# A gated-attention and MLP kernel on one core: a whole-sequence decay pass with a scheduled pipeline, rewritten as six hand-ordered rounds of four units with paired heads

## The chip, the core and the metric

The kernel runs on one core of a Trainium2 chip. The engines named in the profile are PE (matrix multiply; PEld is its weight load), DVE (vector), ACT (activation functions), POOL and SP; SP and POOL also issue the DMAs here. The metric is the device time in microseconds (us). The timed runs of the kernel before gave 297.84, 298.85 and 299.3 us, a median of 298.85 us.

## The reference

```python
batch, n_heads, seq, head_dim = (4, 8, 768, 48)
...
for t in range(S):
    state = alpha[:, :, t, :, None] * state + np.einsum('bhd,bhe->bhde', k[:, :, t], v[:, :, t])
    y[:, :, t] = np.einsum('bhd,bhde->bhe', q[:, :, t], state)
...
x = np.ascontiguousarray(attn_out.transpose(0, 2, 1, 3)).reshape(B * S, H * D)
h = x @ w_in                       # [3072, 384] @ [384, 2048]
g = 0.5 * h * (1.0 + np.tanh(c * (h + 0.044715 * h * h * h)))
return (g @ w_out).astype(np.float32)
```

All inputs and the output are float32. A gated recurrence per batch entry and head is followed by a two-layer MLP with a tanh-GELU on 3072 tokens.

## The kernel before

A unit is 128 time steps of one batch entry, all eight heads: 6 chunks x 4 batch entries = 24 units. Four units with the same chunk form a group, which is 512 tokens for the MLP. Within a unit the recurrence is turned into matmuls. The running sum of log alpha (cum) is a matmul with a triangle of ones; q is scaled by exp(cum), k by exp(-cum); at = k' q' is masked by the triangle (atm); y is atm times v plus q' times the state; and the state moves on as (state + k' v) times the decay of the whole chunk (bend).

**First pass.** For all 24 units, in pairs, POOL issues the alpha loads (L105, rows of 192 bytes in DRAM), ACT takes Ln (L108), PE makes cumla and the chunk's decay (L114, and eight one-column matmuls at L118), DVE stores cum_all (L120) and ACT takes Exp for bend_all (L121). The MLP weights are loaded as float32 by SP and cast by DVE (L127, L159).

**Second pass.** Stage a issues q, k and v on POOL (L190). Stage b takes two Exp on ACT (L200, L202), scales q and k on DVE (L205, L206), casts v on ACT (L208), transposes each head of q and k on PE (L213, L214) and copies both out (L215 ACT, L216 DVE). Stage c does at (L234), the mask (L237, DVE), y (L241, L243), k'v (L245), the state update (L249, L250, DVE), the copy of y to bfloat16 (L255, ACT), its transposes (L259) and their copy (L260, DVE). The MLP of a group is cut into sixteen layer-1 pieces (three matmuls at L275 and a Gelu at L279) and four layer-2 pieces (sixteen matmuls at L286, a copy at L291, a store by SP at L293); up to seven pieces are handed out after each unit.

The program's recording layer sets the order on each engine from this code: it may move an instruction ahead of others by their readiness, and it places the activation-table loads (ACT_TABLE_LOAD) where the function changes between Ln, Exp and Gelu. Each engine then runs its own list strictly in order. A tile pool hands out buffers in turn, and a tile waits until the last reader of its buffer is done.

## Time and profile before

| | |
|---|---|
| median of three timed runs | 298.85 us |
| profiled execution, first to last instruction (the span) | 295.8 us |
| the profiled execution's own time beyond that span | not listed; 298.85 - 295.8 = 3.05 us is the median's distance |
| busy: PE, ACT, DVE, POOL | 224.5, 200.8, 141.3, 87.4 us |
| DMA: read and written | 25.17 and 4.72 MB |
| TensorE clock granted, mean | 0.998 |

A row of instruction groups has the line, engine, operation, tiles (out<-in), sizes and count, then the busy time, the mean of one in ns, the idle time just before them, and what ended most of it. A row of the timeline has start and length in us, engine, line, tiles and count; matmuls are pipelined, so eight in a row take far less than eight times the mean of one. A row of waits has the waiting instruction, what it waited for, the total in us, the number and the longest. A row of a DMA queue has packets, MB, and the time of its packets as a share of sixteen DMA engines in the stretch shown.

### The profile page before, as it was taken

The numbers are of one execution on the slowest core, as the hardware profiler recorded it, in microseconds if no ns is written. First come the engines' busy times: TensorE is split into PE (matmuls) and PEld (weight loads), VectorE is DVE, ScalarE is ACT, GpSimd is POOL, SyncE is SP. The second block draws the span as 40 slices with busy tenths as digits, with TensorE's granted clock in tenths as the row PEclk, the third lists the DMA queues.
The fourth block names the chain that finished last, engine by engine and source line by source line (L and its number), as shares of the span: only waits on it lengthen the run. The fifth ranks groups of instructions, "written<-read, shape, count | busy, mean of one in ns | idle before, by whom it ended". The sixth has DMA issues, their size and how long they took to land.

```text
span 295.8 us, 5241 instructions
## 1 busy us (share of the span) xinstructions
PE 224.5 (76%) x2112; PEld 132.8 (45%) x2112; DVE 141.3 (48%) x274; ACT 200.8 (68%) x301; POOL 87.4 (30%) x114
## 2 busy tenths in 40 slices
PE   0043333332778989899998999999999999999983
PEld 0022212221656535556556555565456644554441
DVE  7183433222599855567548144656243633540011
ACT  0257787978677999996999999945761276304800
POOL 9643321005988758153333213220000000000000
PEclk9999999999999999999999999999999999999999
DMA  7999951002999979373232512241001100011011
GB/s 278 283 187 274 291 126 53 0 1 67 193 187 187 189 144 198 89 181 99 80 82 59 182 53 55 53 109 53 2 1 55 53 2 0 3 53 55 0 53 54
DMA packets 12168, 30.22 MB, mean 102 GB/s; under 512 B 2032, under 2 KB 7152, under 8 KB 11760
## 3 DMA queue, kind: packets, MB, share of 16 engines
q0 software_dynamic: 6144, 18.88, 30.4%
q1 hardware_dynamic: 6000, 11.01, 11.0%
q8 instruction: 16, 0.26, 0.4%
q14 instruction: 8, 0.07, 0.1%
HBM read 25.17 MB, written 4.72 MB: 101 GB/s over the span
## 4 chain that ended last, share of the span: by engine, by line
PE 47%; ACT 34%; DMA 7%; DVE 6%; issue 3%; POOL 1%; SPq 0%; DVEq 0%; POOLq 0%; ACTq 0%
PE acc L286 16%; PE hT L275 15%; ACT gT L279 6%; ACT L279 5%; ACT L108 4%; DMA w_in_f<-in_moe_w_in_dram 4%; ACT qT_ring L215 3%; PE kT_ps L214 3%; PE qT_ps L213 3%; ACT la L108 3%; PE at_ps L234 2%; ACT L200 2%; ACT L202 2%; ACT L121 2%; DVE w_in_sb L127 2%
## 5 line engine op out<-in xcount | busy, mean ns | idle before, releaser
L275 PE MATMUL hT<-xT_all,w_in_sb 128*128 128x512 bf16 x288 | 74.5, 379 | 4.0 <-ACT gT L279 3.8
L286 PE MATMUL acc<-w_out_sb,gT 128*128 128x384 bf16 x384 | 70.8, 326 | 3.0 <-DVE ot L291 2.8
L279 ACT ACTIVATE gT<-hT 128x512 bf16<-128x512 f32 x96 | 55.5, 598 | 16.3 <-PE hT L275 14.2
L286 PEld LDWEIGHTS <-gT 128*128 128x128 bf16 x384 | 36.4, 97 | 28.0 <-issue 4.0
L114 PE MATMUL cumla<-la,ut 128*128 128x384 bf16 x24 | 11.6, 485 | 48.3 <-ACT la L108 39.1
L291 DVE COPY ot<-acc 128x384 f32<-128x384 f32 x24 | 13.3, 555 | 53.6 <-PE acc L286 53.6
L237 DVE TENSOR_TENSOR atm<-at_ps,ut 128x512 bf16<-128x512 f32 x48 | 31.1, 683 | 15.9 <-PE at_ps L234 15.7
L275 PEld LDWEIGHTS <-w_in_sb 128*128 128x128 bf16 x288 | 24.8, 97 | 26.3 <-issue 5.5
L118 PEld LDWEIGHTS <-la 128*48 128x48 bf16 x192 | 9.5, 129 | 55.5 <-issue 55.5
L190 POOL DMA_DIRECT2D q<-in_q_dram x24 | 21.2, 884 | 44.1 <-PE cumla L118 24.1
L120 DVE CAST cum_all<-cumla 128x384 f16<-128x384 f32 x24 | 13.3, 556 | 32.5 <-PE cumla L118 32.5
L190 POOL DMA_DIRECT2D v<-in_v_dram x24 | 21.2, 885 | 25.3 <-ACT v8b L208 21.8
L105 POOL DMA_DIRECT2D a<-in_alpha_dram x24 | 21.5, 900 | 21.3 <-ACT la L108 18.9
L215 ACT COPY qT_ring<-qT_ps 64x1024 bf16<-64x1024 bf16 x24 | 24.1, 1005 | 4.9 <-PE qT_ps L213 4.6
L190 POOL DMA_DIRECT2D k<-in_k_dram x24 | 21.2, 885 | 18.3 <-DVE kp_ring L206 17.4
L208 ACT CAST v8b<-v 128x384 bf16<-128x384 f32 x24 | 12.3, 512 | 18.7 <-PE yps L243 17.9
L216 DVE COPY kT_ring<-kT_ps 64x1024 bf16<-64x1024 bf16 x24 | 16.3, 680 | 17.5 <-PE kT_ps L214 17.1
L108 ACT ACT_TABLE_LOAD x11 | 14.1, 1283 | 13.4 <-DMA a<-in_alpha_dram 13.2
L213 PE MATMUL qT_ps<-ident,qp_ring 128*64 128x128 bf16 x192 | 18.3, 230 | 5.9 <-DVE qp_ring L205 5.3
L205 DVE TENSOR_TENSOR qp_ring<-q,b 128x384 bf16<-128x384 f32 x24 | 13.2, 551 | 14.6 <-PE at_ps L234 5.7
L213 PEld LDWEIGHTS <-qp_ring 128*64 128x64 bf16 x192 | 12.7, 114 | 16.5 <-issue 14.9
L255 ACT CAST x_sb<-yps 128x384 bf16<-128x384 f32 x24 | 11.4, 476 | 12.7 <-PE yps L243 10.6
(49 smaller groups left out, 319.2 us busy)
## 6 DMA issues: line engine op xcount, KB each, us to landing
a<-in_alpha_dram POOLq DMA_DIRECT2D x24, 192.0 KB, 7.2
q<-in_q_dram POOLq DMA_DIRECT2D x24, 192.0 KB, 5.3
k<-in_k_dram POOLq DMA_DIRECT2D x24, 192.0 KB, 5.7
v<-in_v_dram POOLq DMA_DIRECT2D x24, 192.0 KB, 5.2
out_dram<-ot SPq DMA_DIRECT2D x24, 192.0 KB, 1.9
w_in_f<-in_moe_w_in_dram SPq DMA_DIRECT2D x3, 1024.0 KB, 7.4
w_out_f<-in_moe_w_out_dram SPq DMA_DIRECT2D x4, 768.0 KB, 12.4
```

The source lines that it names most:

```text
L105: nc.gpsimd.dma_start(a8[:, i], alpha[b].rearrange("h s d -> s h d")[tsl])
L108: nc.scalar.activation(la8, a8, AF.Ln, scale=float(math.exp(-MU)))
L120: nc.vector.tensor_copy(cum_all[:, tt, :], cumla)
L190: nc.gpsimd.dma_start(t_sb, t_dram[b].rearrange("h s d -> s h d")[tsl])
L213: nc.tensor.transpose(qT_ps[:, h, :], qp[:, h, :], ident)
L215: nc.scalar.copy(qT[0:64], qT_ps)
L216: nc.vector.tensor_copy(kT[0:64], kT_ps)
L237: nc.vector.tensor_tensor(atm, at_ps, ut[:, None, :].to_broadcast([C, 4, C]), op=ALU.mult)
L275: nc.tensor.matmul(hT, w_in_sb[:, j, nt * C:(nt + 1) * C], xsl, start=(j == 0), stop=(j == NKT - 1),)
L279: nc.scalar.activation(gT[:, nt, :], hT, AF.Gelu_apprx_tanh)
L286: nc.tensor.matmul(acc, gT[:, nt, mt * C:(mt + 1) * C], w_out_sb[:, nt, :], start=(nt == 0), stop=(nt == NFT - 1),)
L291: nc.vector.tensor_copy(ot, acc)
```

## The change

The two passes become one. Six groups run in turn through two phases each. In phase A of group g, the layer-2 pieces of group g-1 (sixteen quarter pieces of four matmuls) are interleaved with the attention output of group g (yk) and with the decays of group g+1 (Ln, cum, Exp, scaling). In phase B, the sixteen layer-1 pieces of group g are interleaved with the transposes and the at matrices of group g+1. A helper, _merge, spreads the side work over the main pieces, and the recording layer is told to keep the written order (manual_schedule).

Heads go in pairs: two heads, padded from 48 to 64 columns, fill 128 partitions. A transpose handles two heads (eight per unit in place of sixteen); the two at matmuls of a pair use rows 0-63 and 64-127 of the array; the state of a pair is block diagonal, so q'-state and k'v are four matmuls of 96 columns per unit. Ln and Exp are taken for two units at once and share one table, loaded once per group. v and both weight matrices are cast to bfloat16 by the DMA (on POOL), so the casts on ACT and DVE go away. The first two groups' alpha, q and k are loaded by SP; later groups' by POOL, all in one place, at the start of phase A two groups ahead. PSUM: one two-bank buffer ("ca") for cum and at, two banks ("yk") for transposes, k'v and y, four ("ff") for the MLP.

```diff
-            for pi in range(0, len(units), 2):
...
-    for step in range(NU + 2):
...
+    with ExitStack() as ctx, tc.manual_schedule():
+        _Kernel(ctx, tc, q, k, v, alpha, moe_w_in, moe_w_out, out).run()
...
+def _merge(main, side, first=0.0, last=1.0):
+    lo, hi = first * n, last * n
+    at = [lo + (hi - lo) * (i + 0.5) / m for i in range(m)] if m else []
+    j = 0
+    for i in range(n):
+        while j < m and at[j] <= i:
+            side[j]()
+            j += 1
...
+        self.state = [[const.tile([C, H // 2, 2 * D], BF16, name=f"st{b}_{i}") for i in range(2)]
+                      for b in range(B)]
+        self.NR = 4
+        self.la_ring = [const.tile([C, 2, H, 64], F16, name=f"la{i}") for i in range(self.NR)]
...
+            nc.gpsimd.memset(t[:, :, :, D:64], 0.0)
...
+    def load(self, names, pair, eng):
+        for n in names:
+            dt = F32 if n != "v" else BF16
+            t = self.ld.tile([self.C, 2, self.H, self.D], dt, tag=n + "8", bufs=6 if n == "v" else 4, name=n + "8")
+            for i, (c, b) in enumerate(pair):
+                sl = slice(c * self.C, (c + 1) * self.C)
+                e = eng if n != "v" else self.nc.gpsimd
+                e.dma_start(t[:, i], self.src[n][b].rearrange("h s d -> s h d")[sl])
+                self.u.setdefault((c, b), {})[n] = t[:, i]
+            self.u[pair[0]][n + "pair"] = t
...
+        self.nc.gpsimd.dma_start(
+            self.w_in[:, :, sl], self.w_in_dram.rearrange("(j c) n -> c j n", c=self.C)[:, :, sl])
...
+        self.nc.scalar.activation(self.la_ring[r][:, :, :, 0:self.D], u0["apair"], AF.Ln)
...
+        cum = u0["cum"] = self.ps.tile([self.C, 2, 512], F32, tag="ca", name="cum")
+        for i in range(2):
+            nc.tensor.matmul(cum[:, i, 0:H * D], self.ut_h, la[:, i, :, 0:D], start=True, stop=True)
+            for p in range(H // 2):
+                nc.tensor.matmul(cum[:, i, H * D + p:H * D + p + 1],
+                                 la[:, i, 2 * p:2 * p + 2, :].rearrange("t h d -> t (h d)"),
+                                 self.ones, start=True, stop=True, skip_group_check=True)
...
+        b8 = self.wk.tile([self.C, 2, H * D], BF16, tag="b8", name="b8")
+        binv8 = self.wk.tile([self.C, 2, H * D], BF16, tag="binv8", name="binv8")
+        bend = self.grp.tile([self.C, 2, H // 2], F32, tag="bend", bufs=6, name="bend")
+        nc.scalar.activation(b8, cum[:, :, 0:H * D], AF.Exp)
+        nc.scalar.activation(binv8, cum[:, :, 0:H * D], AF.Exp, scale=-1.0)
+        nc.scalar.activation(bend, cum[:, :, H * D:H * D + H // 2], AF.Exp)
+        qp, kp = self.qp_ring[r], self.kp_ring[r]
+        nc.vector.tensor_tensor(qp[:, :, :, 0:D], u0["qpair"],
+                                b8.rearrange("t i (h d) -> t i h d", h=H), op=ALU.mult)
+        nc.vector.tensor_tensor(kp[:, :, :, 0:D], u0["kpair"],
...
+            ps = self.ps.tile([C, 2, H // 2, C], BF16, tag="yk", bufs=2, name="qkT_ps")
+            for j, s in enumerate((u["qp"], u["kp"])):
+                for p in range(H // 2):
+                    nc.tensor.transpose(
+                        ps[:, j, p, :], s[:, 2 * p:2 * p + 2, :].rearrange("t h d -> t (h d)"), self.ident)
+            nc.vector.tensor_copy(t, ps)
...
+        at = self.ps.tile([C, 2, H // 2, C], F32, tag="ca", name="at")
+        for p in range(H // 2):
+            for o in range(2):
+                sl = slice(64 * o, 64 * o + 64)
+                nc.tensor.matmul(at[:, o, p, :], kT[sl, p, :], qT[sl, p, :], start=True, stop=True)
+        atm = u["atm"] = self.grp.tile([C, 2, H // 2, C], BF16, tag="atm", bufs=6, name="atm")
+        for o in range(2):
+            nc.vector.tensor_tensor(atm[:, o], at[:, o],
+                                    self.ut[:, None, :].to_broadcast([C, H // 2, C]), op=ALU.mult)
...
+        kv = self.ps.tile([C, H // 2, 2 * D], F32, tag="yk", bufs=2, name="kv")
+        for p in range(H // 2):
+            nc.tensor.matmul(kv[:, p, :], u["kp"][:, 2 * p:2 * p + 2, :].rearrange("t h d -> t (h d)"),
+                             u["v"][:, 2 * p:2 * p + 2, :].rearrange("t h d -> t (h d)"),
+                             start=True, stop=True)
+        for o in range(2):
+            ps, fs = slice(64 * o, 64 * o + 64), slice(D * o, D * o + D)
+            acc = kv[ps, :, fs]
+            if c > 0:
+                s = self.wk.tile([C, H // 2, D], F32, tag=f"stmp{o}", name="stmp")
+                nc.vector.tensor_tensor(s[ps], acc, old[ps, :, fs], op=ALU.add)
+                acc = s[ps]
+            nc.vector.tensor_tensor(new[ps, :, fs], acc,
+                                    u["bend"][ps, :, None].to_broadcast([64, H // 2, D]), op=ALU.mult)
...
+        yps = self.ps.tile([C, H, D], F32, tag="yk", bufs=2, name="yps")
+        if c > 0:
+            st = self.state[b][c % 2]
+            for p in range(H // 2):
+                nc.tensor.matmul(yps[:, 2 * p:2 * p + 2, :], u["qT"][:, p, :], st[:, p, :],
+                                 start=p == 0, stop=False, skip_group_check=True)
+        for h in range(H):
+            nc.tensor.matmul(yps[:, h, :], u["atm"][:, h % 2, h // 2, :], u["v"][:, h, :],
+                             start=c == 0, stop=True, skip_group_check=True)
+        x = self.wk.tile([C, H * D], BF16, tag="x", name="x")
+        nc.scalar.copy(x, yps.rearrange("t h d -> t (h d)"))
...
+            ps = self.ps.tile([C, self.NKT, C], BF16, tag="yk", bufs=2, name="xT_ps")
+            for j in range(self.NKT):
+                nc.tensor.transpose(ps[:, j, :], x[:, j * C:(j + 1) * C], self.ident)
+            nc.vector.tensor_copy(xT[:, :, i, :], ps)
...
+            h = self.ps.tile([C, N * C], F32, tag="ff", bufs=4, name="hT")
+            for j in range(self.NKT):
+                nc.tensor.matmul(h, self.w_in[:, j, nt * C:(nt + 1) * C],
+                                 xT[:, j].rearrange("p g t -> p (g t)"),
+                                 start=j == 0, stop=j == self.NKT - 1)
+            nc.scalar.activation(gT[:, nt, :], h, AF.Gelu_apprx_tanh)
...
+                acc[mt] = self.ps.tile([C, self.d_model], F32, tag="ff", bufs=4, name="acc")
+            for nt in range(part * 4, part * 4 + 4):
+                nc.tensor.matmul(acc[mt], gT[:, nt, mt * C:(mt + 1) * C], self.w_out[:, nt, :],
+                                 start=nt == 0, stop=nt == self.NFT - 1)
+            if part == self.NFT // 4 - 1:
+                ot = self.wk.tile([C, self.d_model], F32, tag="ot", name="ot")
+                nc.vector.tensor_copy(ot, acc[mt])
+                c, b = group[mt]
+                r = b * self.S + c * C
+                nc.sync.dma_start(self.out[r:r + C, :], ot)
...
+        self.act_set(LN_EXP_SET)
+        for p in pairs[0]:
+            self.load("aqk", p, nc.sync)
+        for i in range(self.NR):
+            self.pads(i)
+        for p in pairs[0]:
+            self.load("v", p, nc.gpsimd)
+        for b in range(self.B):
...
+        for p in pairs[1]:
+            self.load("a", p, nc.sync)
+        for i in range(4):
+            self.load_w_in(i, 4)
+        for p in pairs[1]:
+            self.load("qk", p, nc.sync)
+            self.load("v", p, nc.gpsimd)
...
+        for f in (ln[0], ln[1], cum[0], exp[0]):
+            f()
+        for cb in pairs[0][0]:
+            self.t_qk(cb)
+        cum[1]()
+        exp[1]()
+        for cb in pairs[0][1]:
+            self.t_qk(cb)
+        for cb in G[0]:
+            self.attn(cb)
...
+            side = []
+            if more:
+                if g + 2 < len(G):
+                    side.append(lambda: [self.load("aqkv", p, nc.gpsimd) for p in pairs[g + 2]])
+                ln, cum, exp = decays(pairs[g + 1])
+                side += [lambda: self.act_set(LN_EXP_SET), ln[0]]
+                side += [lambda: self.yk(G[g][0], xT, 0), ln[1]]
+                side += [lambda: self.yk(G[g][1], xT, 1), cum[0], exp[0]]
+                side += [lambda: self.yk(G[g][2], xT, 2)]
+                side += [lambda: self.yk(G[g][3], xT, 3), cum[1], exp[1]]
+                side += [lambda cb=cb: self.t_qk(cb) for cb in G[g + 1]] if DMA_QK else []
+            else:
+                side += [lambda i=i: self.yk(G[g][i], xT, i) for i in range(4)]
+            if g == 0:
+                side.append(lambda: [self.load_w_out(i, 4) for i in range(4)])
+            main = self.layer2(G[g - 1], gT_prev) if g else []
+            _merge(main, side, 0.0, 0.8)
+            side = []
+            if more:
+                for cb in G[g + 1]:
+                    if not DMA_QK:
+                        side.append(lambda cb=cb: self.t_qk(cb))
+                    side.append(lambda cb=cb: self.attn(cb))
+            _merge(self.layer1(xT, gT), side, 0.1, 1.0)
...
+    def yk(self, cb, xT, i):
+        self.kv(cb)
+        self.y(cb, xT, i)
```

Three places show how the order changed. The first is ACT at the program's start. Before:

```order
L108 ACT_TABLE_LOAD
L108 ACTIVATE la_148<-a_145 128x768
L108 ACTIVATE la_177<-a_174 128x768
L121 ACT_TABLE_LOAD
L121 ACTIVATE bend_all<-cumla,bias_end 48x8 x2
L108 ACT_TABLE_LOAD
L108 ACTIVATE la_206<-a_203 128x768
L121 ACT_TABLE_LOAD
```

And now (la is Ln of alpha; b and binv are the two Exp; x is the copy of y):

```order
L111 ACT_TABLE_LOAD
L120 ACTIVATE la_99<-a_112 128x16x48
L120 ACTIVATE la_100<-a_121 128x16x48
L141 ACTIVATE b_197<-cum 128x768
L142 ACTIVATE binv_198<-cum 128x768
L143 ACTIVATE bend<-cum 128x8
L141 ACTIVATE b_238<-cum 128x768
L142 ACTIVATE binv_239<-cum 128x768
L143 ACTIVATE bend<-cum 128x8
L111 ACT_TABLE_LOAD
L120 ACTIVATE la_101<-a_156 128x16x48
L219 CAST x<-yps 128x384
```

Only the first group's two pairs now pass before the second group's Ln; that Ln (la_101) stands ahead of the first copy of y, and the second pair's Ln (la_100) ahead of the first pair's Exp.

The second place is the issue of loads at the start. Before, POOL held all alpha loads and then q, k and v. Now SP has:

```order
L93 DMA a_112<-in_alpha_dram 128x8x48 x2
L93 DMA q_115<-in_q_dram 128x8x48 x2
L93 DMA k_118<-in_k_dram 128x8x48 x2
L93 DMA a_121<-in_alpha_dram 128x8x48 x2
L93 DMA q_124<-in_q_dram 128x8x48 x2
L93 DMA k_127<-in_k_dram 128x8x48 x2
L93 DMA a_156<-in_alpha_dram 128x8x48 x2
L93 DMA a_159<-in_alpha_dram 128x8x48 x2
L93 DMA q_166<-in_q_dram 128x8x48 x2
L93 DMA k_169<-in_k_dram 128x8x48 x2
L93 DMA q_175<-in_q_dram 128x8x48 x2
L93 DMA k_178<-in_k_dram 128x8x48 x2
```

and POOL, behind its zeroing of the pads:

```order
L93 DMA v_142<-in_v_dram 128x8x48 x2
L93 DMA v_145<-in_v_dram 128x8x48 x2
L100 DMA w_in<-in_moe_w_in_dram 128x3x512 x4
L93 DMA v_172<-in_v_dram 128x8x48 x2
L93 DMA v_181<-in_v_dram 128x8x48 x2
L93 DMA a_318<-in_alpha_dram 128x8x48 x2
L93 DMA q_321<-in_q_dram 128x8x48 x2
L93 DMA k_324<-in_k_dram 128x8x48 x2
L93 DMA v_327<-in_v_dram 128x8x48 x2
L93 DMA a_330<-in_alpha_dram 128x8x48 x2
L93 DMA q_333<-in_q_dram 128x8x48 x2
L106 DMA w_out<-in_moe_w_out_dram 128x4x384 x4
```

SP's first twelve loads serve group 0, the next twelve group 1; POOL's a_318 to q_333 (and k_336, v_339, left out) serve group 2 and stand ahead of w_out. Each reuses a buffer of group 0, so it waits for that group's Ln or scaling.

The third place is DVE in phase A, for one unit. Before (two units overlapped by the scheduler):

```order
L249 TENSOR_TENSOR stmp<-kv,state_b_85 48x384
L205 TENSOR_TENSOR qp_ring_98<-q_1020,b_1145 128x8x48
L250 TENSOR_TENSOR state_b_85<-stmp,bend_all 48x384
L206 TENSOR_TENSOR kp_ring_102<-k_1021,binv_1146 128x8x48
L249 TENSOR_TENSOR stmp<-kv,state_b_87 48x384
```

and now:

```order
L145 TENSOR_TENSOR qp_105<-q_661,b_1236 128x16x48
L147 TENSOR_TENSOR kp_109<-k_664,binv_1237 128x16x48
L200 TENSOR_TENSOR stmp<-kv,st_0_95 64x192
L202 TENSOR_TENSOR st_1_96<-stmp,bend 64x4x48
L200 TENSOR_TENSOR stmp<-kv,st_0_95 64x192
L202 TENSOR_TENSOR st_1_96<-stmp,bend 64x4x48
```

The scaling of a coming pair (qp, kp) now stands ahead of the third unit's state update, and that update is four half-partition instructions in place of two.

More of the change, by code (lines that the diff above doesn't have):

```diff
@@ L2 @@
-import math
-import os
-from contextlib import ExitStack
 import concourse.bass as bass
@@ L8 @@
 from concourse import mybir
-from concourse._compat import with_exitstack
-from concourse.masks import make_upper_triangular
+from concourse.masks import make_identity, make_upper_triangular
 BF16 = mybir.dt.bfloat16
+F16 = mybir.dt.float16
 F32 = mybir.dt.float32
@@ new lines, with kernel @@
+LN_EXP_SET = 6
+DMA_QK = False
+DMA_X = False
+def kernel(tc, q, k, v, alpha, moe_w_in, moe_w_out, out):
+    from contextlib import ExitStack
+    with ExitStack() as ctx, tc.manual_schedule():
+        _Kernel(ctx, tc, q, k, v, alpha, moe_w_in, moe_w_out, out).run()
+def _merge(main, side, first=0.0, last=1.0):
+    n, m = len(main), len(side)
+    lo, hi = first * n, last * n
[5 more added lines that the diff above has]
+            j += 1
+        main[i]()
+    while j < m:
+        side[j]()
+        j += 1
```

375 lines of the change are left out of this document (120 added, 255 removed).

## The prediction

> **What bounds the kernel now.** I read the page's span and slices first, then busy time by stretch, then the waits.
>
> ```profile
> span 295.8 us, 5241 instructions
> PE   0043333332778989899998999999999999999983
> DMA  7999951002999979373232512241001100011011
> ...
> 0.00:78.00 78.00, 23.40 (x240) 14.30 (x241) 30.78 (x62) 51.25 (x71) 32.03 (x52) 1.00 0.61 158
> 78.00:292.00 214.00, 201.08 (x1872) 118.49 (x1871) 109.92 (x212) 149.50 (x231) 55.35 (x63) 1.00 0.35 83
> ...
> PE cumla L114 <- ACT la L108: 39.1, 10, 15.4
> POOL q L190 <- PE cumla L118: 24.1, 1, 24.1
> ```
>
> The slices show two stages. In the stretches (busy us of PE, PEld, DVE, ACT, POOL; then clock, DMA share, GB/s), PE is busy 23 of the first 78 us, waiting for Ln on ACT (39.1 us in all), while POOL's q loads wait 24.1 us for the decay pass. From 78 us PE is busy 201 of 214 us: 35.7 us per group of four units, PE-bound. The granted clock is 1.00 in both.
>
> **Prices.** The first block groups instructions (mean ns just before the second bar); the second is the timeline.
>
> ```profile
> L275 PE MATMUL hT<-xT_all,w_in_sb 128*128 128x512 bf16 x288 | 74.5, 379 | 4.0 <-ACT gT L279 3.8
> L286 PE MATMUL acc<-w_out_sb,gT 128*128 128x384 bf16 x384 | 70.8, 326 | 3.0 <-DVE ot L291 2.8
> L279 ACT ACTIVATE gT<-hT 128x512 bf16<-128x512 f32 x96 | 55.5, 598 | 16.3 <-PE hT L275 14.2
> L237 DVE TENSOR_TENSOR atm<-at_ps,ut 128x512 bf16<-128x512 f32 x48 | 31.1, 683 | 15.9 <-PE at_ps L234 15.7
> L216 DVE COPY kT_ring<-kT_ps 64x1024 bf16<-64x1024 bf16 x24 | 16.3, 680 | 17.5 <-PE kT_ps L214 17.1
> L249 DVE TENSOR_TENSOR stmp<-kv,state_b 48x384 f32<-48x384 f32 x24 | 13.0, 541 | 0.0
> L205 DVE TENSOR_TENSOR qp_ring<-q,b 128x384 bf16<-128x384 f32 x24 | 13.2, 551 | 14.6 <-PE at_ps L234 5.7 <-DMA q<-in_q_dram 5.2 <-PE qT_ps L213 1.1
> L108 ACT ACTIVATE la<-a 128x768 bf16<-128x768 f32 x12 | 10.0, 841 | 0.1
> L108 ACT ACT_TABLE_LOAD x11 | 14.1, 1283 | 13.4 <-DMA a<-in_alpha_dram 13.2
> L279 ACT ACT_TABLE_LOAD x14 | 18.0, 1283 | 0.3
> ...
> 275.06 1.49 PE L275 MATMUL hT<-xT_all,w_in_sb 128*128 128x512 bf16 x6
> 282.46 2.76 PE L286 MATMUL acc<-w_out_sb,gT 128*128 128x384 bf16 x16 [0.65 <-DVE ot L291]
> 85.31 0.38 PE L245 MATMUL kv<-v8b,kp_ring 128*48 128x48 bf16 x8
> 87.20 0.63 PE L213 MATMUL qT_ps<-ident,qp_ring 128*64 128x128 bf16 x8 [0.47 <-DVE qp_ring L205]
> 88.31 0.18 PE L243 MATMUL yps<-state_b,qT_ring 128*128 128x48 bf16 x1
> 88.34 0.18 PE L241 MATMUL yps<-v8b,atm 128*128 128x48 bf16 x1
> 20.90 0.48 PE L118 MATMUL cumla<-ones_col,la 128*48 128x1 bf16 x8
> 81.35 0.18 PE L243 MATMUL yps<-state_b,qT_ring 128*128 128x48 bf16 x1
> 81.57 0.48 ACT L255 CAST x_sb<-yps 128x384 bf16<-128x384 f32 x1 [0.36 <-PE yps L243]
> 82.11 0.34 PE L259 MATMUL xT_ps<-ident,x_sb 128*128 128x128 bf16 x3
> ```
>
> The step between matmuls in a row: layer 1 (1.49 - 0.38)/5 = 0.222; layer 2 (2.76 - 0.33)/15 = 0.162; transposes (0.63 - 0.34)/5 = 0.058, from eight against three; y 0.025; k'v (0.38 - 0.18)/7 = 0.028; one column (0.48 - 0.18)/7, about 0.045 us.
>
> **A steady group after the change.** PE: 48 layer-1 matmuls 10.7; 64 layer-2 10.4; 32 transposes 1.8; 32 at between 0.9 (the two heads of a pair truly side by side) and 1.8, taken 1.7 since each half's weights are loaded in its own instruction; 16 k'v and 16 q'-state of 96 columns between 0.028 and 0.058 each, taken 0.045, 1.4; 32 y 0.8; 12 x transposes 0.7; four cum of 384 columns with four one-column matmuls each, 4 x (0.16 + 0.18) = 1.4. Sum 28.9 us. The same prices for the old group (64 transposes, 64 y, 32 k'v) give 21.1 + 3.7 + 1.8 + 1.6 + 0.9 + 0.7 = 29.8 us, of which 35.7 was made: 5.9 us were waits.
>
> The new waits: within a unit PE issues y and at once the transposes of x, which need ACT's copy. The old rows show 82.11 - 81.35 = 0.76 us from the last y to them; then only unrelated work hid it. PE now stands behind it, and the layer-2 pieces behind PE's head cannot pass. The transposes also take k'v's bank, which DVE frees after three half-partition instructions of 192 columns: between 0.27 (half of 541) and 0.54 each, near 0.35, so 1.05 + 0.2 after k'v, 0.9 after y. Two units at 0.9, the third behind qp and kp of a pair (twice some 0.95: 384 columns take 0.55, two units at once save one fixed part) at 1.5, the fourth 1.1: 4.4 us, bounds 3 (ACT's copy alone, 4 x 0.76) and 8. Hand-overs between phases 1.5. Group: 35 us, no gain, though the work is less. DVE's work in it: eight masks 5.5, four copies of transposes 2.7, four scalings 3.8, sixteen state halves 5.6, four x copies and four of acc 3.6, in all 21 us. ACT's: sixteen Gelus 9.6, two table loads 2.6, two Ln and four Exp of 768 columns 5.0, four x copies 1.9, in all 19. Both lie beside PE's 29. In phase B, where that cover is thinnest, a Gelu (0.60) still fits under its three matmuls (0.67).
>
> Removed here at no gain: the casts of v, and the table loads for Gelu (14) and around it, on engines with slack. Those of the first pass (11 for Ln, as many for Exp, 1.28 us each) lay between its matmuls; they go with it and are no term of their own.
>
> From the first layer-2 matmul to the end: four groups 4 x 35 = 140; last group's phase A without k'v and decays 10.4 + 2.2 + 3 = 15.6; its layer 1, 11.7; last layer 2 with the Gelu's tail, 11.2; last copy and store, as now 295.8 - 292.0 = 3.8. **182 us.**
>
> **The start**, which replaces 78 us and the first group, hangs on the loads.
>
> ```profile
> q0 software_dynamic: 491, 1.52, 103.8%
> ...
> q1 hardware_dynamic: 619, 0.93, 106.1%
> ...
> q0 software_dynamic: 46, 0.19, 69.9%
> q1 hardware_dynamic: 58, 0.09, 37.6%
> ...
> q0 software_dynamic: 92, 0.31, 67.5%
> q1 hardware_dynamic: 93, 0.14, 37.4%
> ...
> q1 hardware_dynamic: 110, 0.81, 100.9%
> ...
> 0.74 1.33 SPq L93 DMA_DIRECT2D w_in_f<-in_moe_w_in_dram  x3
> 19.71 3.11 SPq L130 DMA_DIRECT2D w_out_f<-in_moe_w_out_dram  x4
> ```
>
> The queue rows are five stretches: 12-20 us (POOL's alpha alone), 25.5-28 (SP's w_out alone), 28-29 and 34-36 (both), and 5-7 (SP's w_in alone, 99 of its packets 8 KB). POOL's 192-byte rows run at 1.52 MB/8 us = 190 GB/s, 1.03 us per 192 KB load, in packets of about 3 KB (16 rows), 8 x 16 x 1.038/491 = 0.27 us each. SP's packets are single rows (1536 bytes). With both backlogged the packet counts are nearly equal, 58 to 46 and 93 to 92: the turn goes by packet, not by bytes. SP's new loads have 192-byte rows, 64 per engine and load. If each is a packet, one SP load takes 64 x 0.27/1.3 = 13 us while POOL has work. Alone it takes between 1.0 (bytes as POOL's) and 4.1 us (64 x the 0.065 us of a 1536-byte packet: 2.5 x 16 x 1.06/619); I take 1.2 while SP issues (0.44 us for 128 rows, 0.78 for 512) and 1.03 when several stand queued, nearer the row of equal row length.
>
> In order. POOL's first v moves at about 7.5 us (it zeroes twelve pads first); SP has landed 4.6 loads by then. POOL's backlog: eight v, two alpha, w_in: 10.3 + 9.2 = 19.5 us (a cast's price is not in the trace; between the uncast bytes, 8.4 for 3.1 MB at 374 GB/s, and twice that; near the low end), to 27; SP gets 1.5 loads. ACT stands at the second Ln, which needs loads 7 and 8: 29. Then Ln, Exp, scaling release POOL's next loads, moving at 33.8; loads 9 to 12 have just landed. Group 0's second pair: scaling, transposes, four at (each behind the last one's masks, 2 x 0.68 + 0.6, one "ca" buffer): 47. POOL meanwhile moves fourteen loads and w_out, 23.6 us, to 57.4; SP gets 1.8 loads, so the fourteen needed for ACT's next Ln, and with it the copy of y behind it, are there only then. Loads 15 to 20 and two of POOL's between: 65.6. Scaling, third and fourth unit: layer 1 starts at 70. Group 3's loads on POOL hold loads 21 to 24 until 77.5; qp and kp stand ahead of the at copies on DVE: 80.3. The rest of layer 1, eleven pieces with transposes and at, 11: **91**.
>
> Span 91 + 182 = 273; with the 3.05 us that lie between this span and the median: **276 us**, a ratio of 0.92.
>
> **A rule on the queues.** The Trainium skill's "DMA: Bandwidth & Descriptors" (section on queues, rings and completion order) states that each engine goes round the queues packet by packet. The trace agrees for long packets (58 to 46); for single 192-byte rows no run here shows it. By shares of time instead, the sum is the first rival's.
>
> **Rivals.** (1) *The turn goes by time or bytes*, so SP's short rows travel abreast. For it: the mixed stretches move more than POOL alone. Against: the counts above. All the 15.7 MB due before layer 2 (24 SP loads 4.7, sixteen of group 2 3.1, eight v 1.6, weights 6.3) then travel at the (0.19 + 0.09)/1 us = 280 GB/s of 28-29 us in 56 us; the compute chain gives the last of group 0's loads at 27 (7.4 more at twice 1.2, and 2 to land), 18 to layer 1 (scaling 1.9, transposes 2, four at 8, four units 6), layer 1 15, and 4 for late k and w_out pieces: 64. 64 + 182 + 3 = **249 us**.
>
> (2) *Slower: a 192-byte row of SP costs much more than its bytes.* Some 20 of the 24 loads move outside POOL's bursts, so each us more per load costs 20 us. The old time is reached with 22 us more, at 2.2 us per load (0.034 us per row); at the 4.1 of a full packet price the time is 276 + 60 = **336 us**. For it: the only single-row packets of SP seen cost 0.065. Against: 8 KB ones cost 2 x 16 x 1.009/99 = 0.33, five times as much for 5.3 times the bytes, so time goes mostly by bytes.
>
> (3) *PE drains at each change of row tiling*, before and after at.
>
> The Trainium skill's "TensorEngine Tiling (Array Packing)" (key properties) says that changing the tiling mode drains the array. No run here shows it.
>
> A drain costs at most a matmul's length less its step, (0.23 - 0.06) = 0.17 us, twice per unit, 48 times: 8 us, **284 us**. For it, nothing in the trace; the old at uses all 128 rows.
>
> That the change doesn't do what it says: the written order is kept in the list of instructions, so only the pairs' concurrency is open, 0.8 us per group, priced above.
>
> **Numbers.** Forecast 0.49 (own range 262 to 292, from SP's turn at 1 to 1.5 rows, casts at once to twice the bytes, and waits of 3 to 8 us per group), rival 1 0.30, rival 2 0.12, rival 3 0.09. The forecast and rivals 1 and 3 are faster; of rival 2, 0.02 lies so near its threshold that the time is within 0.5%, which a measurement of this kernel can hardly tell from no change. Faster 0.88, same 0.02, slower 0.10. The range 243 to 296 holds rivals 1 and 3 and the forecast.
>
> **What would show it.** Right: SP's first-twelve loads landing in two bunches with a gap while POOL's queue is full; ACT's second and third Ln waiting on DMA; layer 1 starting near 70 us; groups of 35 us later; DVE and ACT below 65% in them; waits of the x transposes on x and stmp near 0.9 us. Wrong: SP's loads landing evenly beside POOL's, layer 1 before 50 us (rival 1); SP's loads apart by more than 2 us with POOL idle (rival 2); a PE gap of 0.1 us or more around each at block (rival 3); steady groups below 32 or above 38 us, which would mean that my waits are mis-sized.

## The result: 266.4 us, 0.888 of the time before

| | before | the change |
|---|---|---|
| median of the timed runs | 298.7 us | 266.4 us (263.2 to 267.3) |
| profiled execution's span | 295.8 us | 264.8 us |
| first layer-1 matmul, first layer-2 matmul | | 66.1 and 92.7 us |
| one steady group of four units | 35.7 us | 32.5 us |

The ratio is 0.888, with a 95% interval of 0.882 to 0.893. The forecast was 276 us. Some runs took longer at a lower granted clock than others of their kernel (one of four of the change and of experiment 3, two in experiment 2, three in experiment 4), and the medians here hold them too.

Below are the head of the changed kernel's page, its DMA queues, and the shares by engine of its chain that ended last; the last row has these shares for the kernel before.

```profile
span 264.8 us, 3965 instructions
PE   1040332303807988899888998799986999889994
DMA  8999999999988032990329900010000000011011
q0 software_dynamic: 31744, 14.95, 40.3%
q1 hardware_dynamic: 28416, 9.44, 19.4%
PE 57%; SPq 24%; DVE 7%; DMA 5%; ACT 3%; issue 3%; ACTq 0%; DVEq 0%
...
PE 47%; ACT 34%; DMA 7%; DVE 6%; issue 3%; POOL 1%; SPq 0%; DVEq 0%; POOLq 0%; ACTq 0%
```

PE still idles for most of the first ten slices, and now the DMA engines are busy 80% or more in all of them: the start is bound by loads. Where the chain before went 34% through ACT, it now goes 24% through SP's queue (SPq), which issues the first two groups' loads. The next fence has the stretch from the start of one layer 2 to the next of the changed kernel (busy us of PE, PEld, DVE, ACT, POOL; clock, DMA share, GB/s), and PE's waits within it (us, times, longest).

```profile
125.42:157.89 32.47, 29.13 (x275) 17.25 (x273) 20.66 (x40) 18.77 (x31) 14.11 (x16) 1.00 0.65 110
PE xT_ps L225 <- ACT x L219: 2.6, 4, 0.7
PE yps L213 <- DVE xT L226: 0.4, 1, 0.4
```

The steady part is bound by PE: 29.1 of 32.5 us, and 3.0 us of waits that have a name. The start is told by ACT's Ln and DVE's scaling of q and k, the instructions that need the loads (timeline of the changed kernel: start, length, and in brackets the idle time before it and its releaser).

```profile
12.92 0.84 ACT L120 ACTIVATE la<-a 128x768 f16<-128x768 f32 x1 [7.07 <-DMA a<-in_alpha_dram]
38.49 0.84 ACT L120 ACTIVATE la<-a 128x768 f16<-128x768 f32 x1 [16.83 <-DMA a<-in_alpha_dram]
61.75 0.96 DVE L147 TENSOR_TENSOR kp<-k,binv 128x768 bf16<-128x768 f32 x1 [7.02 <-DMA k<-in_k_dram]
74.08 0.96 DVE L145 TENSOR_TENSOR qp<-q,b 128x768 bf16<-128x768 f32 x1 [8.30 <-DMA q<-in_q_dram]
79.04 0.96 DVE L147 TENSOR_TENSOR kp<-k,binv 128x768 bf16<-128x768 f32 x1 [4.00 <-DMA k<-in_k_dram]
...
66.08 0.59 PE L236 MATMUL hT<-xT,w_in 128*128 128x512 bf16 x1
66.89 3.19 PE L236 MATMUL hT<-xT,w_in 128*128 128x512 bf16 x7 [0.22 <-issue]
70.72 1.46 PE L236 MATMUL hT<-xT,w_in 128*128 128x512 bf16 x6
80.66 0.61 PE L177 MATMUL at<-qkT 64*128 64x128 bf16 x8 [8.48 <-DVE qkT L166]
81.20 2.74 PE L236 MATMUL hT<-xT,w_in 128*128 128x512 bf16 x6
92.70 2.77 PE L251 MATMUL acc<-w_out,gT 128*128 128x384 bf16 x16
```

Each of these scalings and Lns stands until a DMA of SP has landed. The last k comes at 79 us; PE had begun layer 1 at 66 and stopped for 8.5 us in the middle of it. The at block at 80.66 does not need this k itself: it needs DVE's copy of its own unit's transposes (L166, 79.92 us), and on DVE that copy stands behind the scaling of this k.

### The profile page after: what moved, and what is told of

Read it like the earlier page. It is cut to its first block, busy times and chain, and to the rows that moved or that the text cites. A ratio compares the mean times of both kernels' runs of the same rounds, so it can differ in the third digit from the quotient of the medians.

```text
span 264.8 us, 3965 instructions
## 1 busy us (share of the span) xinstructions
PE 184.5 (70%) x1589; PEld 108.6 (41%) x1600; DVE 117.7 (44%) x225; ACT 110.9 (42%) x179; POOL 74.1 (28%) x102
## 4 chain that ended last, share of the span: by engine, by line
PE 57%; SPq 24%; DVE 7%; DMA 5%; ACT 3%; issue 3%; ACTq 0%; DVEq 0%
SPq L93 24%; PE hT L236 22%; PE acc L251 22%; DMA k<-in_k_dram 5%; PE qkT_ps L164 3%; ACT x L219 3%; PE at L177 3%; PE xT_ps L225 2%; DVE kp L147 2%; DVE qkT L166 2%; DVE qp L145 1%; PE yps L216 1%; PE yps L213 1%; PE cum L128 1%; PE kv L191 1%
## 5 line engine op out<-in xcount | busy, mean ns | idle before, releaser
L236 PE MATMUL hT<-xT,w_in 128*128 128x512 bf16 x277 | 71.4, 392 | 0.7 <-issue 0.2
L251 PE MATMUL acc<-w_out,gT 128*128 128x384 bf16 x384 | 69.0, 330 | 0.0
L180 DVE TENSOR_TENSOR atm<-at,ut 128x512 bf16<-128x512 f32 x48 | 30.9, 686 | 18.5 <-PE at L177 18.5
L236 PEld LDWEIGHTS <-w_in 128*128 128x128 bf16 x288 | 26.7, 100 | 28.4 <-issue 3.2
L219 ACT CAST x<-yps 128x384 bf16<-128x384 f32 x24 | 11.5, 477 | 50.0 <-PE yps L216 50.0
L145 DVE TENSOR_TENSOR qp<-q,b 128x768 bf16<-128x768 f32 x12 | 11.5, 958 | 35.7 <-DMA q<-in_q_dram 20.5
L166 DVE COPY qkT<-qkT_ps 128x1024 bf16<-128x1024 bf16 x24 | 16.6, 691 | 19.0 <-PE qkT_ps L164 19.0
L93 POOL DMA_DIRECT2D a<-in_alpha_dram x16 | 14.3, 905 | 28.4 <-ACT la L120 23.6
L164 PE MATMUL qkT_ps<-ident,qp 128*128 128x128 bf16 x96 | 10.7, 242 | 15.0 <-DVE qp L145 15.0
L177 PE MATMUL at<-qkT 64*128 64x128 bf16 x192 | 10.6, 237 | 13.4 <-DVE qkT L166 8.5
L147 DVE TENSOR_TENSOR kp<-k,binv 128x768 bf16<-128x768 f32 x12 | 11.4, 953 | 14.5 <-DMA k<-in_k_dram 14.5
L93 POOL DMA_DIRECT2D k<-in_k_dram x16 | 14.1, 884 | 12.9 <-DVE st L202 7.0
```

The source lines that it names most:

```text
L93: e.dma_start(t[:, i], self.src[n][b].rearrange("h s d -> s h d")[sl])
L145: nc.vector.tensor_tensor(qp[:, :, :, 0:D], u0["qpair"], b8.rearrange("t i (h d) -> t i h d", h=H), op=ALU.mult)
L147: nc.vector.tensor_tensor(kp[:, :, :, 0:D], u0["kpair"], binv8.rearrange("t i (h d) -> t i h d", h=H), op=ALU.mult)
L164: nc.tensor.transpose(ps[:, j, p, :], s[:, 2 * p:2 * p + 2, :].rearrange("t h d -> t (h d)"), self.ident)
L166: nc.vector.tensor_copy(t, ps)
L177: nc.tensor.matmul(at[:, o, p, :], kT[sl, p, :], qT[sl, p, :], start=True, stop=True)
```

## The experiments

Times are medians of four runs, shown beside 266.4 us of the change; the span is that of the profiled run.

### 1. The first loads on one queue

```diff
-            self.load("aqk", p, nc.sync)
+            self.load("aqk", p, nc.gpsimd)
...
-            self.load("a", p, nc.sync)
+            self.load("a", p, nc.gpsimd)
...
-            self.load("qk", p, nc.sync)
+            self.load("qk", p, nc.gpsimd)
```

> The a, q and k of the first two groups are issued on POOL's queue again, in the same order, and nothing else is changed. Theory (the two queues take turns by packet, and a packet of SP's is one row of 192 bytes): without SP's short packets the one queue moves the first loads in order, so the last k of the second group lands near 45 us instead of 78.9, layer 2 starts at 58 to 65 us instead of 92.7, and the time falls from 266 to between 232 and 240 us. Rival (the DMA engines, busy over 90% up to 60 us, are the bound by the bytes and casts that they move, whichever queue): layer 2 starts within 4 us of 92.7 and the time stays within 4 us of 266.

Measured: **243.2 us** (242.3 to 243.6), ratio to before 0.812 (0.809 to 0.814). Layer 1 starts at 44.5 in place of 66.1 us. This is the timeline of PE in this run.

```profile
44.49 0.59 PE L236 MATMUL hT<-xT,w_in 128*128 128x512 bf16 x1
59.35 0.40 PE L177 MATMUL at<-qkT 64*128 64x128 bf16 x8
64.26 1.46 PE L251 MATMUL acc<-w_out,gT 128*128 128x384 bf16 x4 [4.51 <-DMA w_out<-in_moe_w_out_dram]
66.19 1.44 PE L251 MATMUL acc<-w_out,gT 128*128 128x384 bf16 x4 [0.47 <-DMA w_out<-in_moe_w_out_dram]
```

The second queue cost 23 us: SP's short rows are what made the start late. The time came out 3 us above the range, for two reasons that the rows show. PE was ready for layer 2 at 59.75, but w_out, now the last in the one queue, kept it for 4.5 us and then three times for half a microsecond. And the four quarter pieces after that stop took 1.44 us each, where they take 0.81 in the steady part.

### 2. The third group's loads behind w_out

```diff
-                if g + 2 < len(G):
+                if g > 0 and g + 2 < len(G):
...
                 side.append(lambda: [self.load_w_out(i, 4) for i in range(4)])
+                side.append(lambda: [self.load("aqkv", p, nc.gpsimd) for p in pairs[2]])
```

> The loads of the third group, which POOL issues ahead of w_out while SP's loads of the second group are still under way, are issued behind w_out instead. Theory (SP's loads 13 to 24 lose turns to whatever POOL has): the work that competes with them shrinks by the third group's 2.4 MB, so the last k of the second group lands 8 to 14 us earlier than 78.9, layer 2 starts at 79 to 85 us instead of 92.7, and the time falls by 8 to 14 us to 252 to 258. Rival (SP's loads are late because their buffers come free late or because SP's queue waits for itself): no change beyond 3 us, or a loss, since w_out lands earlier but is not waited for.

Measured: **263.5 us** (260.7 to 266.8; no interval), layer 2 at 87.0 us. The direction was that of the theory, and the start came 5.7 us earlier, about half of the size. The times are divided: 260.7 and 261.2 us (the profiled run) agree with that, 265.7 and 266.8 do not, so the rival's 3 us is not excluded. The rows of the two queues (packets, MB, share) in 34 to 46 us tell why it was only half; first the change, then this run.

```profile
q0 software_dynamic: 2550, 1.65, 90.1%
q1 hardware_dynamic: 2567, 0.48, 37.9%
```

```profile
q0 software_dynamic: 1859, 2.04, 94.6%
q1 hardware_dynamic: 1874, 0.35, 26.8%
```

POOL's queue (q0) is busy in both, and SP's (q1) sends one packet for each of POOL's. With w_out moved ahead, POOL's packets here are longer, so there are fewer of them, and SP gets a quarter fewer turns; it gets them back only from 60 to 75 us (5024 packets for 3803). I had counted the bytes that were moved away and not the packets that give SP its turn. The buffers are not the reason: the change issues the third group's loads from 18.1 to 45.5 us, and the scalings that free their buffers come earlier in each case (the last at 28.4 us), so these loads did not wait for them as the section on the change has it.

### 3. v without the cast

```diff
-            dt = F32 if n != "v" else BF16
+            dt = F32
...
+        vb = self.grp.tile([self.C, 2, H, D], BF16, tag="vb", bufs=6, name="vb")
+        nc.scalar.copy(vb, u0["vpair"])
```

> The cast of v in its DMA is undone: v is loaded as 32-bit rows, and ScalarE writes the 16-bit copy behind the three Exp of its pair. Theory (turn by packet; the v that is cast goes in packets of one row, which the row of the queues between 8 and 12 us shows: 2586 packets for 0.25 MB): with v in long packets POOL's part of the first 12 us needs fewer turns, so SP gets fewer loads in while POOL works on v, but POOL is done with v sooner; the two nearly cancel, and layer 2 starts within 5 us of 92.7. Rival (a cast costs DMA time of its own, about 28 ns a row of 96 bytes on an engine): 24 of the 48 v loads end sooner by some 1 to 2 us each in the first 70 us, and layer 2 starts 5 to 10 us earlier, time 256 to 262. ScalarE has about 0.9 us more per pair, under PE's work in both.

Measured: **264.4 us** (262.5 to 267.5), ratio 0.881 (0.877 to 0.885), layer 2 at 89.9 us: 2.8 earlier, inside the theory's 5 and short of the rival's. What decides is the queues from 14 to 34 us, first of the change, then of this run.

```profile
q0 software_dynamic: 6031, 2.46, 93.6%
q1 hardware_dynamic: 5415, 1.02, 46.7%
```

```profile
q0 software_dynamic: 2216, 3.45, 95.0%
q1 hardware_dynamic: 2217, 0.42, 19.8%
```

With v in long packets the two queues send 2216 and 2217 packets: one for one, while POOL moves eight times SP's bytes. In the change POOL's casts go in single rows of 96 bytes, many short turns, and SP gets 1.02 MB through in place of 0.42. The step at which SP issues its third and fourth k shows it too: it takes 8.71 us in the change and 20.87 us in this run. Later SP has POOL's idle time to itself (5864 packets from 34 to 46 us, where the change has 2567), which is why the end of the start hardly moves.

### 4. A piece of layer 2 between the copy of y and its transposes

```diff
-    def y(self, cb, xT, i):
+    def y(self, cb):
...
         nc.scalar.copy(x, yps.rearrange("t h d -> t (h d)"))
+
+    def xt(self, cb, xT, i):
...
-                side += [lambda: self.yk(G[g][0], xT, 0), ln[1]]
+                side += [lambda: self.yk(G[g][0]), lambda: (self.xt(G[g][0], xT, 0), ln[1]())]
```

> The piece that computes a unit's output and transposes it is split in two, with a quarter of a layer-2 tile between the copy to x and the transposes that read it. Theory (PE stands 0.62 us in each unit before the transposes, because the ScalarE copy is just being made): this wait goes in 20 units of the steady groups; a group falls from 32.5 us to about 30, and the time from 266 to 254 at the best (20 x 0.62 = 12.4 us). Rival (the waits of a unit are one chain over the two buffers that the transposes, kv and the outputs share, so that what is taken from one wait comes back at the next): a group stays within 0.7 us of 32.5 and the time within 4 us of 266. The start (layer 2 at 92.7) is unchanged by both.

Measured: **253.3 us** (247.5 to 255.0; the runs of this kernel spread too far for an interval). The steady group is read from a stretch where nothing else differs:

```profile
122.58:153.01 30.43, 29.09 (x274) 16.81 (x273) 20.49 (x40) 18.78 (x31) 14.11 (x16) 1.00 0.70 117
PE yps L213 <- DVE xT L230: 0.7, 2, 0.5
PE kv L191 <- DVE stmp L200: 0.3, 1, 0.3
```

The wait for x is gone; the same PE work, 29.1 us, now takes 30.4 in place of 32.5. From the first layer 2 to the last phase A four groups take 122.2 us in place of 132.0, and the last phase A 12.9 in place of 15.8: 12.7 of the 13.1 us. The theory holds: the wait was a matter of order alone and did not come back elsewhere.

### 5 and 6. One queue in the order of need, v uncast and cast

Both have the edits of runs 1 and 4. The loads go by need, and the pads are zeroed on DVE. Run 5 has the edit of run 3 as well.

```diff
-            nc.gpsimd.memset(t[:, :, :, D:64], 0.0)
+            nc.vector.memset(t[:, :, :, D:64], 0.0)
...
+        for p in pairs[0] + pairs[1]:
+            self.load("aqkv", p, nc.gpsimd)
         for i in range(4):
             self.load_w_in(i, 4)
+        for i in range(4):
+            self.load_w_out(i, 4)
```

> The edits of the runs before together, and the order of need: all first loads on POOL's queue, unit by unit (alpha, q, k, v of a pair, uncast, then the next pair), then w_in, w_out and only then the third group; the pads are zeroed on VectorE; the x transposes stand a piece behind the copy they read. Theory (the start is set by the order in which one queue brings the bytes, at about 0.98 us per 192 KB): 32 loads of the first two groups have landed at 34 us, w_in at 42 to 45, w_out at 50 to 55; layer 2 starts at 50 to 57 us, and with 30.5 us per steady group the time is 213 to 222 us. Rival (PE's and ScalarE's own chain through the first group, and not the loads, set the 59.8 us at which layer 1 was done in the run with the first loads on POOL): layer 2 starts at 58 to 62 us, time 222 to 230.

> The same kernel as the one-queue run by need, but v is cast in its DMA, as in the change. Theory (a cast goes in packets of one row, about 28 ns for each row of 96 bytes on an engine, 1024 rows of a unit on 16 engines, 1.8 us a unit against 0.98 for the uncast one): the eight v loads ahead of layer 1 take 6.5 us more, layer 2 starts 4 to 7 us later, and the time is 4 to 7 us longer than that of the uncast run. Rival (a cast load moves half the bytes on the written side and costs at most the uncast one): the two are within 1.5 us, the cast one not the slower, since ScalarE also has 0.6 us less work per pair.

Measured: **222.3 us** for the uncast v, ratio 0.744 (0.741 to 0.747), and **219.9 us** for the cast one, ratio 0.736 (0.733 to 0.738). Layer 2 starts at 59.3 and 58.7 us, so of run 5 the rival comes nearer: w_out is no longer waited for, but layer 1, at 43.4 and 42.7, starts only 1 to 2 us sooner than in run 1. Of run 6 the theory falls: the cast is the cheaper one, by 2.4 us, more than the rival's 1.5. Of the 1.8 us between the two spans 0.6 lie ahead of layer 2; the rest lies behind it, where run 5 also has ACT's copies of v. The second Ln of each, which stands behind all four loads of the first pair and its own two, gives the price (first run 5, then run 6):

```profile
7.50 0.84 ACT L120 ACTIVATE la<-a 128x768 f16<-128x768 f32 x1 [5.49 <-DMA a<-in_alpha_dram]
15.93 0.84 ACT L120 ACTIVATE la<-a 128x768 f16<-128x768 f32 x1 [7.58 <-DMA a<-in_alpha_dram]
```

```profile
7.42 0.84 ACT L120 ACTIVATE la<-a 128x768 f16<-128x768 f32 x1 [5.41 <-DMA a<-in_alpha_dram]
15.24 0.84 ACT L120 ACTIVATE la<-a 128x768 f16<-128x768 f32 x1 [6.97 <-DMA a<-in_alpha_dram]
```

Eight loads lie between the two Lns: 8.43 us uncast, 1.05 each; with two of them cast 7.82, so a cast load of one unit's v takes (7.82 - 6 x 1.05)/2 = 0.75 us, an estimate that takes the DMA engines as full between the two Lns, which they are not quite. The 28 ns per row from which I had 1.8 us came from a stretch where two queues' packets overlapped (shares of 115% and 71%), and a packet's time there is not its price.

### 7. The halves of an at block one after the other

```diff
-        for p in range(H // 2):
-            for o in range(2):
+        for o in range(2):
+            for p in range(H // 2):
```

> The change as it stands, but the eight matmuls of a unit's at block are issued by halves: four on rows 0 to 63, then four on rows 64 to 127, instead of alternating. Theory (the step of 0.023 us between them comes from the two halves of the array working side by side): matmuls of one half follow each other at 0.045 to 0.055 us, the block goes from 0.40 to 0.55 to 0.62 us, and the time rises by 0.15 to 0.2 us in each of 20 units behind the start, 3 to 4.5 us, to 269 to 271 us. Rival (a matmul of 64 rows is short by itself, whatever runs beside it): the block stays at 0.40 us and the time within 1.5 us of 266.

Measured: **266.0 us** (264.8 to 266.9), ratio 0.890 (0.886 to 0.893): the same as the change. PE's timeline of the change, then of this run:

```profile
87.50 1.46 PE L236 MATMUL hT<-xT,w_in 128*128 128x512 bf16 x6
88.90 0.40 PE L177 MATMUL at<-qkT 64*128 64x128 bf16 x8
89.23 1.47 PE L236 MATMUL hT<-xT,w_in 128*128 128x512 bf16 x6
90.53 0.39 PE L164 MATMUL qkT_ps<-ident,qp 128*128 128x128 bf16 x4
```

```profile
87.19 1.46 PE L236 MATMUL hT<-xT,w_in 128*128 128x512 bf16 x6
88.58 0.41 PE L177 MATMUL at<-qkT 64*128 64x128 bf16 x8
```

The block goes from 0.40 to 0.41 us. The order of the halves does not matter, so the short step is not bought by alternating them.

### 8. At over all rows

```diff
-                nc.tensor.matmul(at[:, o, p, :], kT[sl, p, :], qT[sl, p, :], start=True, stop=True)
+                nc.tensor.matmul(at[:, o, p, :], kT[:, p, :], qT[:, p, :], start=True, stop=True)
```

> The change, but each at matmul contracts over all 128 rows (both heads of a pair at once, so the at blocks are sums of two heads and the output is not the reference's; the count, columns and places of the matmuls stay). This prices the split in halves by itself. Theory (a matmul of 64 rows gets out of the way sooner, 0.041 us from one to the next against 0.056 of a full one): the block goes from 0.33 us, start to the next matmul, to 0.44 to 0.47, and the time rises by 0.11 to 0.14 us in each of 24 units where PE is the bound, 2 to 3 us. Rival (PE loses time where the tiling of its rows changes, twice a block, and the split gains less than that): the gaps around the block shrink, and the time falls by up to 8 us.

Measured: **266.5 us** (265.8 to 268.7), ratio 0.891 (0.887 to 0.896): no difference. PE's timeline:

```profile
87.92 1.46 PE L235 MATMUL hT<-xT,w_in 128*128 128x512 bf16 x6
89.22 0.61 PE L176 MATMUL at<-qkT 128*128 128x128 bf16 x8
89.66 1.46 PE L235 MATMUL hT<-xT,w_in 128*128 128x512 bf16 x6
90.96 0.39 PE L164 MATMUL qkT_ps<-ident,qp 128*128 128x128 bf16 x4
```

Read these starts against those of the change above. Six layer-1 matmuls ahead of something with full rows take 1.30 us (89.23 to 90.53, and 89.66 to 90.96). Ahead of the block in halves they take 1.40 (87.50 to 88.90; 1.39 in run 7); ahead of the block over all rows 1.30 (87.92 to 89.22). So there is a gap of 0.10 us where the rows are split, and it goes with the split. Behind the first of the eight, the next layer-1 matmul comes after 0.33 us in halves, 0.44 over all rows; eight steps of a full matmul, (0.61 - 0.22)/7 = 0.056 us, are 0.45, so there is no gap behind them. The halves' steps, (0.40 - 0.217)/7 = 0.026 us (0.217 us being the median of one at matmul), make 0.21 of their 0.33, which leaves some 0.12 us of a gap behind. Both expectations are half right: the split saves 0.24 us of matmuls in a block and gives back 0.22 at its two edges.

### 9. The first loads ahead of the triangles

The three lines that build the two triangles and the identity on POOL move behind the first pair's loads, in the kernel of run 6.

```diff
+        self.load("aqkv", pairs[0][0], nc.gpsimd)
         make_upper_triangular(nc, self.ut_h, val=1.0, diag=True)
...
-        for p in pairs[0] + pairs[1]:
+        for p in [pairs[0][1]] + pairs[1]:
```

> The one-queue kernel by need with v cast, with POOL's loads of the first pair issued ahead of the three triangles and the identity that POOL builds in its first 2.3 us. Theory (the start is a chain from the first loads through ScalarE, VectorE and PE): the first Ln moves from 7.4 to about 5.2 us and the whole start with it, layer 2 from 58.7 to 56 to 57 us, time 217 to 219. Rival (the later loads, at their 1 us each, set layer 1, and they are issued no sooner than the queue takes them): layer 2 stays within 0.7 us of 58.7.

Measured: **219.0 us** (218.8 to 219.6), ratio 0.731 (0.729 to 0.733). The first Ln comes 0.9 us earlier, the second Ln and the start of layer 1 only 0.3 (42.4 for 42.7), as the rival had it in size. It is the fastest kernel of the study. The second Ln and the start of layer 1 in this run:

```profile
14.96 0.84 ACT L117 ACTIVATE la<-a 128x768 f16<-128x768 f32 x1 [7.62 <-DMA a<-in_alpha_dram]
...
42.42 0.59 PE L237 MATMUL hT<-xT,w_in 128*128 128x512 bf16 x1
```

Layer 1 starts 27.46 us behind the second Ln here, and just as long behind it in run 5 (43.39 - 15.93) and run 6 (42.70 - 15.24). Every wait of ACT, DVE and PE between the two is put down to ACT, DVE or PE but one, the first scaling of q, and that one ends 0.03 to 0.04 us behind the Exp that it also needs, in all three runs. So the loads set this start only up to the second pair's alpha, and from there it is the first group's own chain of work.

## Why the prediction was right, and where it was off

**The start: 91 us forecast, 92.7 measured, by the mechanism named, but so close by luck.** The turn goes by packet, and a row of SP is one packet: run 3 shows it to one packet in two thousand from 14 to 34 us, and run 1 that the second queue costs 23 us. The Trainium skill's "DMA: Bandwidth & Descriptors" (section on queues, rings and completion order), whose round by packets the prediction cited, agrees with these counts for 192-byte rows too.

But the stations on the way were off, and the errors cancelled. The second Ln was put at 29 us and came at 12.9; the third at 57.4 and came at 38.5; the at blocks of the first group were to end at 47 and end at 37.6; layer 1 was to start at 70 and starts at 66.1; loads 21 to 24 were due at 77.5, and the last k is there at 79.0. Two steps failed, in opposite directions.

The first is the packets of POOL's backlog. I gave its casts packets of 3 KB and 0.27 us, as alpha has. But v goes in rows of 96 bytes, and w_in in packets of 1 KB (1136 packets, 1.12 MB from 15 to 22 us). These are the change's queues from 8 to 14 us:

```profile
q0 software_dynamic: 3858, 0.39, 115.5%
q1 hardware_dynamic: 2826, 0.54, 68.6%
```

So from 8 to 24 us SP sent 4549 rows, 4.4 loads where I had 1.5, and by 8 us it had already sent 6.1 where I had 4.6 by 7.5; the first group was done early. v's rows are not all of it: in run 3, where v goes in long packets, the second Ln comes at 17.8 us, still 11 ahead of the forecast. What is left there is SP's early start, and gaps in POOL's queue, which I had as full: from 9 to 10 us of run 3 it sends 13 packets and SP 885.

The second is that I let POOL's queue run empty, from 27 to 33.8 us and again at 57.4, so that SP would bring loads 15 to 20 almost alone in 8.2 us. It does not run empty: its share is 90 to 93% in the three stretches from 20 to 60 us and 87% from 60 to 75, and those six loads take 23 us, from 38.5 to 61.8. Against packets of 3 KB (run 3 from 26 to 38 us: 685 of POOL, 683 of SP) a load of SP takes 12 x 1024/683 = 18 us. I had 13, by a divisor of 1.3 for which the prediction gives no row.

**Price of a row of SP.** I took 1.2 and then 1.03 us for a load of SP alone. The queue row from 2 to 5 us of the change shows 0.60 MB in 3 us, 201 GB/s, 0.98 us per load:

```profile
q1 hardware_dynamic: 3184, 0.60, 108.2%
```

So the low end of 1.0 to 4.1 was right, and rival 2 falls by it. (The high end has a slip: 2.5 x 16 x 1.06/619 is 0.069 us, not 0.065, so 64 of them are 4.4 us.)

**Price of a cast.** "Between the uncast bytes and twice that": run 6 shows 0.75 us against 1.05, below the low end.

**The steady group: 35 us forecast, 32.5 measured.** PE's work was right: 28.9 us in the sum, 29.1 measured. DVE and ACT at 64 and 58% lie below the 65% that were forecast. What was mis-sized is the idle time: waits 4.4, measured 3.0, and 1.5 for hand-overs, of which 0.3 is left (32.47 - 29.13 - 3.0). The transposes wait 0.62 to 0.70 us in each unit, and the third and fourth unit, for which I had 1.5 and 1.1 behind the scaling, hardly more than the first. "No gain" was therefore wrong by 2.5 us a group: four groups were 132.0 us in place of 140. The rest of the 182 us was near: last phase A 15.8 (15.6), layer 1 10.4 (11.7), last layer 2 with the tail 14.0 (15.0); together 172.1. So the forecast of 276 was 9.9 us too long here, 1.7 too short at the start, and 1.5 too long in what lies beyond the span (1.56 in place of 3.05 us; the kernel before has 1.8 when a run is set beside its own span, 299.23 beside 297.4, so the 3.05 was mostly the distance between two runs).

**The pairs, and rival 3.** I took 1.7 us per group for the at matmuls, near the price of heads that do not run side by side, and let rival 3 add the drains to that. Measured (the block shown in run 8), a block and the gap ahead of it take 0.10 + 0.33 = 0.43 us, 1.72 per group. The number was right for the wrong reason: the matmuls are cheap (0.026 us a step, near my low bound of 0.9 per group) and the change of row tiling is dear, 0.22 us per block where rival 3 had 0.34. Rival 3's gaps are real, its 8 us are not, because they had been taken by the price of the matmuls already. The Trainium skill's "TensorEngine Tiling (Array Packing)" (key properties) states that a change of the tiling mode drains the array, and run 8 agrees, by the gaps that go with the split; whether the loading of the weights has a part in them no run separates. Run 7 shows that the short step needs no alternation of the halves; why it is short is open.

**Rival 1** (turn by time or bytes) falls by the packet counts. Its price of 249 us is about what run 1 makes possible, 243, once the second queue is gone.

**What stays open.** Which part of the first group's chain behind the second Ln could be shortened in runs 5, 6 and 9, no run tried. Run 2's gain is too small to be sure of.

## What to carry to other kernels

A second queue is no second road: where two queues share the DMA engines packet by packet, the one with short rows starves while the other has long packets; put what is needed first in one queue, in the order of need, and count packets, not bytes, when two queues meet. A reader placed right behind its producer on an in-order engine waits out the other engine's whole latency; one piece of unrelated work between them took 2 us off every 32.5. And a mode that makes an operation cheap (half the rows) has its price at the edges: here, in blocks of eight, the two were equal, and whether longer blocks would gain no run shows.

## What was not expected of the hardware

The granted clock falls to 0.50 after PE has stood still. Rows are stretches of the change (busy us as above; the figure behind POOL's is the clock):

```profile
78.00:80.00 2.00, 0.00 (x0) 0.00 (x0) 0.96 (x2) 0.00 (x0) 0.00 (x0) 0.50 0.39 103
80.00:84.00 4.00, 3.34 (x17) 1.50 (x18) 1.89 (x3) 0.62 (x2) 3.53 (x4) 0.50 0.40 99
```

In run 1 the same happened behind the 4.5 us stop for w_out: 0.50 from 66 to 74 us. A layer-1 matmul then steps at about 0.43 us in place of 0.22, which by these steps cost the change about 2 us and run 1 some 3, an estimate. In the first layer-1 pieces of the change (seven in 3.19 us from 66.9 on, (3.19 - 0.59)/6 = 0.43 each) the step is the same slow one though the clock's row reads 1.00 there; so in the start, the step of a known matmul tells the clock better than the row does. The prediction had read that row of the kernel before as full speed; there the 384-column matmuls of the first pass (L114) took 0.485 us on the mean, as long as the change's in its start (0.48), where the steady part has 0.33.
